# Attention scores and values in seven pieces of 64 keys, on the four quarters of the array

## The chip, the cores and the metric

The kernel runs on one NeuronCore of a Trainium2 chip. A core has TensorE (PE; its weight loads are shown apart as PEld), VectorE (DVE), ScalarE (ACT), GpSimd (POOL) and SyncE (SP, which here only issues transfers), all with their own instruction queues, and 16 DMA engines. The metric is the device time of one execution in microseconds; the times given are medians of several executions.

## The reference

Eight sequences of 448 tokens, 12 heads of 64. Attention with root-mean-square norms on q and k, then a SwiGLU feed-forward layer (FFN) on the joined heads:

```python
def _attn_ref(q, k, v, g_q, g_k):            # (8, 12, 448, 64), g: (64,)
    q_n, k_n = (rmsnorm(q, g_q), rmsnorm(k, g_k))
    scores = np.matmul(q_n, k_n.transpose(0, 1, 3, 2)) / np.sqrt(64)
    attn = np.exp(scores - np.max(scores, axis=-1, keepdims=True))
    attn = attn / (np.sum(attn, axis=-1, keepdims=True) + 1e-09)
    return np.matmul(attn, v)

def _moe_ref(x, w_gate, w_val, w_out, rms_g): # x: (3584, 768), d_ff 1536
    xn = x / rms * rms_g
    g = xn @ w_gate
    silu = g * (1.0 / (1.0 + np.exp(-g)))
    return silu * (xn @ w_val) @ w_out
```

All of it is float32 on the chip; the weights come as float64 and are converted by the kernel.

## The kernel before

Two versions of the computation are in the program: `safe_scores`, which runs unless a flag says that the scores could overflow, and `any_scores` behind the flag. Only `safe_scores` runs in the measurements, and only it is changed.

**Pairs.** Attention goes by pairs of heads, 48 pairs `g` in all, six for each sequence. A pair's 448 keys are 384 "full" ones, laid out as three blocks of 128 (`NK` = 3), and a rest of 64. q and k are turned by TensorE (`turn`, L531 and L535) into `qT` and `kT`, tiles of 128 partitions in which one head takes 64 partitions and the other head the other 64: `own(j)` and `across(j)` are these halves. In a 64-partition half the sum over the head's 64 numbers takes place.

**Scores, transposed.** `score` (L549) makes, for a block of 128 keys and one head, a tile of 128 keys by 448 queries: it contracts over 64 partitions (shape 64\*128 in the profile), so that the two heads use the upper and the lower half of the array. `Exp` on ACT (L553) writes `e`, and takes the key's norm `rs` as its scale per partition, since k itself is turned without it. `rests` does the last 64 keys with both heads in one tile (L579, shape 64\*64: each head has a quarter of the array, on the diagonal); these keys are normalised beforehand, so their `Exp` (L594) has no scale. There is no subtraction of a maximum: the scores are bounded by the norms.

**Values.** `av` is 128 partitions (two heads by 64) by 448 queries in one PSUM bank (pool `ps_m`, one buffer, shared with the turned tiles `tr`). `values` (L601) contracts over 128 keys and writes 64 rows (shape 128\*64), six matmuls a pair; `rests` adds the last keys' (L585) on the two quarters off the diagonal.

**Sums of e.** For the first seven pairs (`direct`) TensorE adds them all with a matrix of ones (L590, L614). From pair 7 on, POOL adds the tiles of each head into `es` (L559, L566), and TensorE adds over the keys with two matmuls (`den`, L614); ACT copies `den` (L621), DVE takes the reciprocal (L622) and multiplies `av` by it (L629) into `x`. The squares of x for the FFN's norm follow on ACT (L634) and POOL (L635).

**Norms of q and k.** `squares` (L488, ACT) for the pair after next, the sums on DVE (L491), `rms_qk` on POOL (L509, and L510, a power of -1/2, into `rs`), and `norm_q` on POOL (L515).

**Order.** Everything is ordered by hand: each engine runs its instructions in the order in which the program writes them. `pe(fn)` writes one step of TensorE's work, advances a counter, and then writes what `after(n, ...)` had put off to that step. The main loop at the end writes, for a pair g above 7: one burst of attention (scores of g with values and sums of g-1), and then the FFN's matmuls of an earlier sequence, item by item (`fill`), with the turns of g+1 between them. So ACT, DVE and POOL get attention work and FFN work in one mixed, fixed order. `load_pair` (three pairs ahead) and `load_v` (two ahead) are written on SP's queue among the transfers of the FFN's weights (L752, L801, L911).

**The FFN.** For the first sequence plain matmuls (L1363, L1101), while the weights are converted: ACT (L765, L766), DVE (L771 to L773) and POOL (L813), piece by piece; for later ones Strassen-like products (`quad`, L1004; outputs L1228 and L1296) in three PSUM buffers (`ps_f`), with sums on DVE and POOL and copies and tanh on ACT (L1023, L1046, L1315). The scores use four other PSUM buffers (`ps_s`), which a score's tile gives back after its `Exp`.

Of the kernel before, what the change touches and what calls it, by code (L numbers as in the profile page):

```python
# [8 lines left out]
F32 = mybir.dt.float32  # L9
# [3 lines left out]
ALU = mybir.AluOpType  # L13
ACT = mybir.ActivationFunctionType
# [4 lines left out]
B, H, S, D = 8, 12, 448, 64  # L19
DM, DF = H * D, 1536  # L20
NT, P = 4, 112
NK, REST = 3, S - 3 * 128
NPAIR = H // 2
# [312 lines left out]
def safe_scores(  # L336
# [20 lines left out]
    nc = tc.nc  # L357
# [16 lines left out]
    st = {}  # L374
# [4 lines left out]
    def after(n, fn):  # L379
        due.append((now["t"] + n, fn))  # L380

    def pe(fn):
        now["t"] += 1
        fn()
        for item in [d for d in due if d[0] <= now["t"]]:
            due.remove(item)
            item[1]()
# [6 lines left out]
    NG = B * NPAIR  # L394
# [4 lines left out]
    def own(j):  # L399
        return slice(j * D, (j + 1) * D)  # L400

    def across(j):
        return own(1 - j)
# [17 lines left out]
    def load_v(g):  # L421
        if g >= NG:
            return
        b, hp = divmod(g, NPAIR)
        vt = st["v", g] = v_pool.tile([128, 2, NK, D], F32, name="vt")
        nc.sync.dma_start(out=vt.rearrange("p h t d -> p h (t d)"),
                          in_=v[b, 2 * hp:2 * hp + 2, FULL].rearrange("h (p t) d -> p h (t d)", t=NK))


    def load_rests(b, i, engine):  # L430
# [44 lines left out]
    def direct(g):  # L475

        return g <= NPAIR

    def squares(g, i):

        if g >= NG:
            return
        n = 2 * NK
        if i == 0:
            st["ms", g] = small.tile([128, 2 * n], F32, name="ms")
        ms = st["ms", g]
        sq = tmp.tile([128, n * D], F32, name="sq", tag="sq", bufs=2)
        nc.scalar.activation(sq, st["qk", g][:, i], ACT.Square)  # L488

        def reduce():  # L490
            nc.vector.tensor_reduce(out=ms[:, i * n:(i + 1) * n], in_=sq.rearrange("p (n d) -> p n d", d=D), axis=AX_X, op=ALU.add)  # L491

        if g <= 1:

            return reduce, lambda: rms_qk(g, slice(i * n, (i + 1) * n))
        after(1, reduce)
        if i == 1:
            if g == 2:

                due[0:0] = [(now["t"] + 2, lambda: rms_qk(g)), (now["t"] + 2, lambda: norm_q(g))]  # L500
                return
            after(2, lambda: rms_qk(g))
            after(2, lambda: norm_q(g))

    def rms_qk(g, cols=slice(0, 4 * NK)):
        if ("rs", g) not in st:
# [5 lines left out]
    def norm_q(g):  # L512
        qn = st["qn", g] = qn_pool.tile([128, 2 * NK * D], F32, name="qn")
        for h in range(2):
            (nc.vector if g <= 2 else nc.gpsimd).tensor_tensor(  # L515
                qn.rearrange("p (t h d) -> p h t d", h=2, d=D)[:, 1 - h], st["qk", g][:, 0].rearrange("p (h t d) -> p h t d", h=2, d=D)[:, h],
                st["rs", g][:, h * NK:(h + 1) * NK].unsqueeze(2).to_broadcast([128, NK, D]), ALU.mult)

    def turn(g, i):

# [20 lines left out]
    def score(g, cs):  # L541

        qT, kT, rs = st["qT", g], st["kT", g], st["rs", g]
        sc = {}
        for c in cs:
            for j in range(2):
                r = across(j)
                ps = sc[c, j] = ps_s.tile([128, 512], F32, name="sc", tag="s")
                nc.tensor.matmul(ps[:, 0:S], lhsT=kT[r, c * 128:(c + 1) * 128], rhs=qT[r, :], start=True, stop=True)  # L549
        for (c, j), ps in sc.items():  # L550
            e = st["e", g, c, j] = e_pool.tile([128, S], F32, name="e")
            n = 2 * NK + c * 2 + 1 - j
            nc.scalar.activation(e, ps[:, 0:S], ACT.Exp, scale=rs[:, n:n + 1])  # L553


        def first():
            for j in range(2):
                es = st["es", g, j] = tmp.tile([128, S], F32, name="es", tag="es", bufs=4)
                nc.gpsimd.tensor_tensor(es, st["e", g, 0, j], st["e", g, 1, j], ALU.add)  # L559

        def more(of):
            for j in range(2):
                r = across(j) if of == "rest" else slice(0, 128)
                e = st["e", g, of] if of == "rest" else st["e", g, of, j]
                es = st["es", g, j]
                nc.gpsimd.tensor_tensor(es[r], es[r], e[r], ALU.add)  # L566

        if NK - 1 in cs and not direct(g):
            n = 3 if g == NPAIR + 1 else 2
            after(n, first)  # L570
            after(n + 2, lambda: more(2))
            after(n + 3, lambda: more("rest"))

    def rests(g):

        if g < NG:
            ps = ps_s.tile([128, 512], F32, name="sc", tag="s")
            for r in (own(0), own(1)):
                nc.tensor.matmul(ps[r, 0:S], lhsT=st["kT", g][r, LAST], rhs=st["qT", g][r, :], start=True, stop=True)  # L579
        if g:  # L580
            b, hp = divmod(g - 1, NPAIR)
            vr, e = st["vr", b][:, hp], st["e", g - 1, "rest"]
            av = st["av", g - 1] = ps_m.tile([128, 512], F32, name="av", tag="m")
            for j in range(2):
                nc.tensor.matmul(av[own(j), 0:S], lhsT=vr[across(j)], rhs=e[across(j)], start=True, stop=False,  # L585
                                 skip_group_check=True)
            if direct(g - 1):
                den = st["den", g - 1] = ps_f.tile([128, 512], F32, name="den", tag="f")
                for j in range(2):
                    nc.tensor.matmul(den[own(j), 0:S], lhsT=ones[across(j)], rhs=e[across(j)], start=True, stop=False,  # L590
                                     skip_group_check=True)
        if g < NG:
            e = st["e", g, "rest"] = e_pool.tile([128, S], F32, name="e")
            nc.scalar.activation(e, ps[:, 0:S], ACT.Exp)  # L594

    def values(g):

# [6 lines left out]
    def sums(g):  # L604


        b, hp = divmod(g, NPAIR)
        if direct(g):
            den, terms = st.pop(("den", g)), [[st["e", g, c, j] for j in range(2)] for c in range(NK)]
        else:  # L610
            den, terms = ps_s.tile([128, 512], F32, name="den", tag="s"), [[st.pop(("es", g, j)) for j in range(2)]]
        for i, pair in enumerate(terms):
            for j, term in enumerate(pair):
                nc.tensor.matmul(den[own(j), 0:S], lhsT=ones, rhs=term, start=not direct(g), stop=(i == len(terms) - 1),  # L614
                                 skip_group_check=True)
        rd = tmp.tile([128, S], F32, name="rd", tag="rd", bufs=1)
        if direct(g):
            nc.vector.reciprocal(rd, den[:, 0:S])
        else:

            nc.scalar.copy(rd, den[:, 0:S])  # L621
            nc.vector.reciprocal(rd, rd)  # L622
        half, c = divmod(hp, 3)
        if c == 0:
            st["x", b, half] = x_pool.tile([128, 3, S], F32, name="x")
        if hp == 0:
            st["ss", b] = tmp.tile([128, S], F32, name="ss", tag="ss", bufs=1)
        x, ss, av = st["x", b, half][:, c, :], st["ss", b], st.pop(("av", g))
        nc.vector.tensor_tensor(x, av[:, 0:S], rd, ALU.mult)  # L629
        soon = g == NPAIR - 1  # L630
        if hp == 0:
            after(3, lambda: nc.scalar.activation(ss, x, ACT.Square))
        else:
            after(1 if soon else 3, lambda: nc.scalar.activation(rd, x, ACT.Square))  # L634
            after(1 if soon else 4, lambda: (nc.gpsimd.tensor_tensor(ss, ss, rd, ALU.add), st.update({("summed", b): hp})))  # L635
        st.pop(("e", g, "rest"))
        for c in range(NK):
            for j in range(2):
                st.pop(("e", g, c, j))
        for key in ("qk", "v", "qT", "kT", "rs", "ms"):  # L640
            st.pop((key, g))


    def rms_x(b):
# [806 lines left out]
    ones = const.tile([128, D], F32, name="ones")  # L1451
# [71 lines left out]
    for g in range(NG + 1):  # L1523
# [45 lines left out]
                bound()  # L1569
            continue  # L1570

        pe(lambda: (rests(g), score(g, (0,)) if g < NG else None))
        if g == NPAIR + 1:
            pe(lambda: rms_x(0))
        pe(lambda: values(g - 1))
        load_v(g + 2)
        if g == NPAIR + 1:
            pe(lambda: score(g, (1,)))
            pe(lambda: norm_x(0))
            pe(lambda: score(g, (2,)))  # L1580
        pe(lambda: sums(g - 1))
        if g == NPAIR + 1:
            begin(0, 15)
        elif g < NG:
            pe(lambda: score(g, (1, 2)))
        st["block"] = now["t"]
        if hp:
            fill()
# [60 lines left out]
```

## Time and profile before

| | |
|---|---|
| median of 3 runs | 1577.93 us (1576.43 to 1578.04) |
| the profiled execution's own time | 1576.27 us |
| its span, first to last instruction | 1574.4 us |
| TensorE busy | 1544.4 us (98% of the span) |
| scores L549 / values L601 | 138.0 / 118.8 us of TensorE |
| DVE / POOL / ACT busy | 979.7 / 724.0 / 472.7 us |
| granted TensorE clock | 0.998 |

The profile is one execution, as the hardware recorded it. A group line gives line, engine, operation, output and inputs with shapes, the number of instructions, then busy time and mean duration of one in ns, then the engine's idle time in front of them with what ended it. Durations overlap where an engine is pipelined: matmuls that run side by side each show their full length. An f32 matmul shows as two passes, each with its own weight load, so L549's 288 matmuls are 576 rows. A timeline line gives start and length in us, and after "x" how many instructions were merged.

### The profile page before, as it was taken

The numbers are of one execution on the slowest core, as the hardware profiler recorded it, in microseconds if no ns is written. First come the engines' busy times: TensorE is split into PE (matmuls) and PEld (weight loads), VectorE is DVE, ScalarE is ACT, GpSimd is POOL, SyncE is SP. The second block draws the span as 40 slices with busy tenths as digits, with TensorE's granted clock in tenths as the row PEclk, the third lists the DMA queues.
The fourth block names the chain that finished last, engine by engine and source line by source line (L and its number), as shares of the span: only waits on it lengthen the run. The fifth ranks groups of instructions, "written<-read, shape, count | busy, mean of one in ns | idle before, by whom it ended". The sixth has DMA issues, their size and how long they took to land.

```text
span 1574.4 us, 23664 instructions
## 1 busy us (share of the span) xinstructions
PE 1544.4 (98%) x7916; PEld 1193.3 (76%) x7916; DVE 979.7 (62%) x1697; ACT 472.7 (30%) x955; POOL 724.0 (46%) x718
## 2 busy tenths in 40 slices
PE   8999999999999999999999999999999999999997
PEld 4344445777856888788887888668888788999997
DVE  6889889668754565854558544534549544573454
ACT  6746564232222222223222222322322222101000
POOL 6867887544423443464435643354544542021003
PEclk9999999999999999999999999999999999999999
DMA  7648574775789979785557855484556755578665
GB/s 208 214 142 266 169 236 139 251 238 195 252 264 292 307 225 301 237 253 172 153 163 214 267 160 156 142 262 144 151 146 210 233 172 141 161 259 261 175 196 186
DMA packets 313414, 327.10 MB, mean 208 GB/s; under 512 B 83652, under 2 KB 310212, under 8 KB 313284
## 3 DMA queue, kind: packets, MB, share of 16 engines
q1 hardware_dynamic: 312356, 325.30, 67.2%
q8 instruction: 65, 1.06, 0.3%
q14 instruction: 65, 0.53, 0.1%
q10 hardware_dynamic: 800, 0.20, 0.1%
q0 software_dynamic: 128, 0.00, 0.0%
HBM read 271.62 MB, written 53.77 MB: 207 GB/s over the span
## 4 chain that ended last, share of the span: by engine, by line
PE 75%; DVE 9%; issue 1%; DMA 1%; POOL 0%; ACT 0%; SPq 0%; DVEq 0%; POOLq 0%; ACTq 0%
PE ff L1004 42%; PE ff L1296 10%; PE sc L549 6%; PE av L601 5%; PE ff L1228 5%; PE sc L579 2%; PE den L614 2%; PE ff L1101 2%; PE tr L531 1%; DVE l L1171 1%; DVE top L772 1%; DVE rd L622 1%; DVE top L773 1%; DVE top L771 1%; DVE xs L684 1%
## 5 line engine op out<-in xcount | busy, mean ns | idle before, releaser
L1004 PE MATMUL ff<-x,w 128*128 128x224 f32 x1866 | 380.4, 354 | 0.0
L1004 PEld LDWEIGHTS ff<-x,w 128*128 128x128 f32 x1866 | 348.5, 190 | 15.6 <-issue 11.1
L559 POOL TENSOR_TENSOR es<-e 128x448 f32<-128x448 f32 x82 | 91.2, 1133 | 433.4 <-ACT e L553 433.4
L1004 PE MATMUL ff<-xs,w 128*128 128x224 f32 x1392 | 284.6, 353 | 3.2 <-DVE w L926 2.9
L1004 PEld LDWEIGHTS ff<-xs,w 128*128 128x128 f32 x1392 | 261.9, 190 | 4.9 <-issue 4.1
L566 POOL TENSOR_TENSOR es<-es,e 64x448 f32<-64x448 f32 (+1 forms) x164 | 197.3, 1213 | 6.3
L622 DVE RECIPROCAL rd<-rd 128x448 f32<-128x448 f32 x41 | 121.1, 2952 | 99.6 <-ACT rd L621 99.6
L553 ACT ACTIVATE e<-sc,rs 128x448 f32<-128x448 f32 x288 | 161.2, 634 | 49.8 <-PE sc L549 47.4
L549 PE MATMUL sc<-qT,kT 64*128 64x448 f32 x576 | 138.0, 572 | 1.9 <-ACT e L553 0.7
L601 PE MATMUL av<-e,vt 128*64 128x448 f32 x576 | 118.8, 548 | 0.0
L510 POOL TENSOR_TENSOR rs<-ms,mhalf 128x12 f32<-128x12 f32 (+1 forms) x50 | 115.9, 2318 | 4.2
L549 PEld LDWEIGHTS sc<-qT,kT 64*128 64x128 f32 x576 | 53.9, 185 | 82.5 <-issue 68.5
L1016 DVE TENSOR_TENSOR cc<-ff,u 128x448 f32<-128x448 f32 x84 | 52.4, 624 | 101.2 <-PE ff L1004 98.0
L1296 PE MATMUL ff<-w,l 128*128 128x192 f32 x578 | 110.0, 329 | 3.7 <-DVE l L1171 2.6
L1363 PE MATMUL ff<-x,w 128*128 128x448 f32 x288 | 111.8, 541 | 0.0
L1296 PEld LDWEIGHTS ff<-w,l 128*128 128x128 f32 x578 | 95.4, 190 | 9.7 <-DVE l L1171 4.5
L601 PEld LDWEIGHTS av<-e,vt 128*64 128x64 f32 x576 | 37.1, 136 | 75.6 <-issue 74.9
L1363 PEld LDWEIGHTS ff<-x,w 128*128 128x128 f32 x288 | 53.3, 190 | 50.8 <-issue 49.0
L1023 ACT ACTIVATE th<-c 128x224 f32<-128x224 f32 x42 | 16.3, 389 | 226.8 <-DVE c L1016 226.8
L1268 POOL TENSOR_TENSOR y<-y,c 128x384 f32<-128x384 f32 x10 | 12.2, 1216 | 151.9 <-DVE y L1337 143.0
L635 POOL TENSOR_TENSOR ss<-ss,rd 128x448 f32<-128x448 f32 x40 | 46.4, 1160 | 77.3 <-ACT rd L634 77.3
L813 POOL TENSOR_TENSOR w<-top,raw 128x384 int32<-128x384 int32 x63 | 66.5, 1069 | 25.6 <-issue 8.4
(199 smaller groups left out, 2337.0 us busy)
## 6 DMA issues: line engine op xcount, KB each, us to landing
w<-kept SPq DMA_DIRECT2D x512, 192.0 KB, 3.5
w<-kept_q SPq DMA_DIRECT2D x323, 192.0 KB, 3.5
w<-kept_o SPq DMA_DIRECT2D x136, 192.0 KB, 3.6
kept<-w SPq DMA_DIRECT2D x91, 192.0 KB, 3.7
kept_q<-w SPq DMA_DIRECT2D x57, 192.0 KB, 3.1
qk<-in_q_dram SPq DMA_DIRECT2D x48, 192.0 KB, 3.4
qk<-in_k_dram SPq DMA_DIRECT2D x96, 96.0 KB, 3.5
vt<-in_v_dram SPq DMA_DIRECT2D x48, 192.0 KB, 3.5
```

What stands on the lines that cost most here:

```text
L510: nc.gpsimd.tensor_tensor(st["rs", g][:, cols], ms, mhalf[:, cols], ALU.pow)
L549: nc.tensor.matmul(ps[:, 0:S], lhsT=kT[r, c * 128:(c + 1) * 128], rhs=qT[r, :], start=True, stop=True)
L553: nc.scalar.activation(e, ps[:, 0:S], ACT.Exp, scale=rs[:, n:n + 1])
L559: nc.gpsimd.tensor_tensor(es, st["e", g, 0, j], st["e", g, 1, j], ALU.add)
L566: nc.gpsimd.tensor_tensor(es[r], es[r], e[r], ALU.add)
L601: nc.tensor.matmul(av[own(j), 0:S], lhsT=vt[:, j, c], rhs=st["e", g, c, j], start=False, stop=(c == NK - 1), skip_group_check=True)
L622: nc.vector.reciprocal(rd, rd)
L813: nc.gpsimd.tensor_tensor(data(key).bitcast(I32), top, lo, ALU.add)
L1004: nc.tensor.matmul(bank[:, w * HT:(w + 1) * HT], lhsT=wt[:, c * 128:(c + 1) * 128], rhs=x[:, c, :], start=onto is None and w == c == 0, st ...
L1228: nc.tensor.matmul(ps, lhsT=left_o(b, which, LEFT_O[name], c), rhs=data(("wo", b, name, c)), start=first and c == 0, stop=c == NFP - 1, sk ...
L1296: nc.tensor.matmul(ps, lhsT=a[:, j, :], rhs=data(key)[:, n % 2 * HW:(n % 2 + 1) * HW], start=start and j == 0, stop=j == KG - 1, skip_grou ...
L1363: nc.tensor.matmul(bank[w][:, 0:S], lhsT=data(key)[:, c * 128:(c + 1) * 128], rhs=st["x", 0, half][:, c, :], start=half == c == 0, stop=ha ...
```

## The change

From pair 7 on, each pair's 448 keys are done in seven pieces of 64 keys (`PARTS`), as the rest was: for a piece, two score matmuls on the diagonal quarters (both heads in one PSUM tile), and two value matmuls of the pair before on the other quarters (`step`). Since a piece's `e` tile has keys of both heads on its partitions, the tile of sums `es` is one per pair, over all 128 partitions, and the two `den` matmuls (`totals`) contract over 64 partitions on the values' quarters. `totals` stands after two steps and writes the copy and the reciprocal; the multiplication (`weigh`) comes after the seventh step. The `Exp` has no scale; instead ACT multiplies k in place by `rs` (`norm_k`, six Copies of 128x64 for each pair, in two groups, three and four steps after the squares). v is loaded per head by two transfers, in an order that puts the keys of piece i and i + 3 of a block in the two halves. The first seven pairs (0 to 6) stay as they were, and their last half meets the new form at pair 7, whose scores are written without values beside them; after the last pair the values of pair 47 are written without scores.

The core of the diff; "..." marks what is left out:

```diff
@@ load_v
-        nc.sync.dma_start(out=vt.rearrange("p h t d -> p h (t d)"),
-                          in_=v[b, 2 * hp:2 * hp + 2, FULL].rearrange("h (p t) d -> p h (t d)", t=NK))
+        rows = vt.rearrange("p h t d -> p h (t d)")
+        if direct(g):
+            nc.sync.dma_start(out=rows, in_=v[b, 2 * hp:2 * hp + 2, FULL].rearrange("h (p t) d -> p h (t d)", t=NK))
+            return
+        for h in range(2):
+            nc.sync.dma_start(out=rows[across(h)], in_=v[b, 2 * hp + h, FULL].rearrange("(f p t) d -> p f (t d)", f=2, t=NK))
@@ squares
             after(2, lambda: norm_q(g))
+            if not direct(g):
+                for half in range(2):
+                    after(3 + half, lambda half=half: norm_k(g, half))
...
+    def norm_k(g, half):
+        for n in range(NK * half, NK * (half + 1)):
+            block = st["qk", g][:, 1, n * D:(n + 1) * D]
+            nc.scalar.activation(block, block, ACT.Copy, scale=st["rs", g][:, 2 * NK + n:2 * NK + n + 1])
@@ score: the POOL sums of two es tiles are gone (now later_sums)
...
@@ sums: for the direct pairs alone; its second half is weigh
-        rd = tmp.tile([128, S], F32, name="rd", tag="rd", bufs=1)
-        if direct(g):
-            nc.vector.reciprocal(rd, den[:, 0:S])
-        else:
-            nc.scalar.copy(rd, den[:, 0:S])
-            nc.vector.reciprocal(rd, rd)
...
+    PARTS = 2 * NK + 1
+
+    def keys_of(i):
+        at = i % NK * 128 + i // NK * D if i < 2 * NK else NK * 128
+        return slice(at, at + D)
+
+    def scores(g, i):
+        ps = ps_s.tile([128, 512], F32, name="sc", tag="s")
+        for r in (own(0), own(1)):
+            nc.tensor.matmul(ps[r, 0:S], lhsT=st["kT", g][r, keys_of(i)], rhs=st["qT", g][r, :], start=True, stop=True)
+        return ps
+
+    def exps(g, i, ps):
+        e = st["e", g, i] = e_pool.tile([128, S], F32, name="e")
+        nc.scalar.activation(e, ps[:, 0:S], ACT.Exp)
+
+    def weighted(g, i):
...
+        for j in range(2):
+            r = across(j)
+            vt = st["vr", b][r, hp] if i == PARTS - 1 else st["v", g][r, i // NK, i % NK]
+            nc.tensor.matmul(st["av", g][own(j), 0:S], lhsT=vt, rhs=st["e", g, i][r], start=i == 0, stop=i == PARTS - 1,
+                             skip_group_check=True)
+
+    def step(g, i):
+        ps = scores(g, i) if g < NG else None
+        weighted(g - 1, i)
+        if ps is not None:
+            exps(g, i, ps)
+
+    def totals(g):
+        es, den = st.pop(("es", g)), ps_s.tile([128, 512], F32, name="den", tag="s")
+        for j in range(2):
+            nc.tensor.matmul(den[own(j), 0:S], lhsT=ones[across(j)], rhs=es[across(j)], start=True, stop=True)
+        rd = st["rd"] = tmp.tile([128, S], F32, name="rd", tag="rd", bufs=1)
+        nc.scalar.copy(rd, den[:, 0:S])
+        nc.vector.reciprocal(rd, rd)
+
+    def later_sums(g, n):
+        def first():
+            st["es", g] = tmp.tile([128, S], F32, name="es", tag="es", bufs=2)
+            nc.gpsimd.tensor_tensor(st["es", g], st["e", g, 0], st["e", g, 1], ALU.add)
+            more(2)
+        def more(*parts):
+            for i in parts:
+                nc.gpsimd.tensor_tensor(st["es", g], st["es", g], st["e", g, i], ALU.add)
+        after(n, first)
+        after(n + 2, lambda: more(3, 4))
+        after(n + 3, lambda: more(5, 6))
@@ main loop, pairs above 7 (and the values after the last pair)
-        pe(lambda: (rests(g), score(g, (0,)) if g < NG else None))
...
-        pe(lambda: values(g - 1))
-        load_v(g + 2)
...
-        pe(lambda: sums(g - 1))
...
-        elif g < NG:
-            pe(lambda: score(g, (1, 2)))
+            pe(lambda: [step(g, i) for i in (0, 1)])
+            pe(lambda: (totals(g - 1), step(g, 2)))
+            load_v(g + 2)
+            pe(lambda: [step(g, i) for i in (3, 4)])
+            pe(lambda: ([step(g, i) for i in (5, 6)], weigh(g - 1, 2)))
+            if g < NG:
+                later_sums(g, 2)
```

## The prediction

> **What bounds the kernel now.** I read the page first: busy shares and the costliest groups. TensorE is busy nearly all the time and no other engine comes near it.
>
> ```profile
> PE 1544.4 (98%) x7916; PEld 1193.3 (76%) x7916; DVE 979.7 (62%) x1697; ACT 472.7 (30%) x955; POOL 724.0 (46%) x718
> ...
> L549 PE MATMUL sc<-qT,kT 64*128 64x448 f32 x576 | 138.0, 572 | 1.9 <-ACT e L553 0.7
> L601 PE MATMUL av<-e,vt 128*64 128x448 f32 x576 | 118.8, 548 | 0.0
> ```
>
> The reader is to see that the two groups which the change cuts up (scores L549, values L601) hold 257 us of TensorE time and that almost nothing is waited for in front of them. So what counts is how much TensorE time one pair's attention takes, and whether anything new makes TensorE wait. Next, the timeline of TensorE for one middle pair (start, us, line, operation, number of passes; an f32 matmul shows as two passes):
>
> ```profile
> 600.08 0.59 PE L579 MATMUL sc<-qT,kT 64*64 64x448 f32 x2
> 600.10 0.59 PE L585 MATMUL av<-e,vr 64*64 64x448 f32 x2
> 600.51 0.54 PE L579 MATMUL sc<-qT,kT 64*64 64x448 f32 x2
> 600.52 0.54 PE L585 MATMUL av<-e,vr 64*64 64x448 f32 x2
> 601.00 1.02 PE L549 MATMUL sc<-qT,kT 64*128 64x448 f32 x4
> 601.95 2.48 PE L601 MATMUL av<-e,vt 128*64 128x448 f32 x12
> 604.25 0.92 PE L614 MATMUL den<-es,ones 128*64 128x448 f32 x4
> 605.11 1.77 PE L549 MATMUL sc<-qT,kT 64*128 64x448 f32 x8
> 606.81 0.46 PE L1004 MATMUL ff<-x,w 128*128 128x224 f32 x1
> ```
>
> The burst lasts 606.81 - 600.08 = 6.73 us; 38 of the 40 bursts from pair 8 on last 6.73 to 6.75. Its first 0.92 us already do what the change wants everywhere: scores on the diagonal quarters and values on the others start within 0.02 us of each other, twice. The weight loads of the values inside the burst give the pace of a set (passes that run side by side), and an earlier burst shows quarters following quarters:
>
> ```profile
> 602.38 0.14 PEld L601 LDWEIGHTS av<-e,vt 128*64 128x64 f32 x2 [0.23 <-issue]
> 602.75 0.14 PEld L601 LDWEIGHTS av<-e,vt 128*64 128x64 f32 x2 [0.23 <-issue]
> 603.13 0.14 PEld L601 LDWEIGHTS av<-e,vt 128*64 128x64 f32 x2 [0.23 <-issue]
> ```
>
> ```profile
> 75.78 0.59 PE L579 MATMUL sc<-qT,kT 64*64 64x448 f32 x2
> 75.79 0.59 PE L585 MATMUL av<-e,vr 64*64 64x448 f32 x2
> 76.20 0.54 PE L579 MATMUL sc<-qT,kT 64*64 64x448 f32 x2
> 76.22 0.54 PE L585 MATMUL av<-e,vr 64*64 64x448 f32 x2
> 76.59 0.92 PE L590 MATMUL den<-e,ones 64*64 64x448 f32 x4
> 77.44 2.48 PE L601 MATMUL av<-e,vt 128*64 128x448 f32 x12
> ```
>
> A set takes 0.375 us once the shape stays the same (602.38, 602.75, 603.13). The first set of a shape takes 0.42 (75.78 to 76.20), and the last before another shape 0.85 - 0.375 = 0.475 (two den sets, 76.59 to 77.44). Each change of shape thus costs about 0.15 us, and a burst has five.
>
> **The change, part by part.** *Burst.* Today's work is 2 + 2 + 6 + 2 + 4 = 16 sets: 6.0 us plus 0.73 for the changes of shape. After, seven steps of two sets each, and two den sets on the values' quarters: again 16 sets on the busier quarters, all 64x64. So the array does no less work; only the changes of shape go: 0.42 + 14 x 0.375 + 0.475 = 6.15. I take 6.2, a gain of 0.53 per burst. From both sides: if only the switches inside went and a set of four took the 0.41 to 0.42 of the first one, 16 x 0.415 = 6.64 (gain 0.09); at 16 x 0.375 = 6.0 the gain is 0.73.
>
> The rule that speaks against this is in the Trainium skill, TensorE: Matmul & The Clock Gate, "Packing small matmuls — row/col tiling": a weight load overlaps running matmuls only when its row group differs. In the new burst both row groups always run, so by it each set would show a load; with this case's 64x64 loads of 0.131 us, 16 x (0.375 + 0.131) = 8.1 us, and 40 bursts would cost 55 us more. The trace speaks against it: the den load that uses the same rows is issued at 76.22, while L579's passes of 76.20 to 76.74 run, and den's first pass starts at 76.59, 0.39 after.
>
> *ACT in the burst.* Seven exps as before (0.52 to 0.58 apart), the den copy (0.53) and at most one or two tanh: about 5 us of 6.2. Score tiles use four PSUM buffers; by these rows the den copy ends about 3.4 us into the burst and the step that reuses its buffer starts at about 4.2. It is covered with 0.75 us to spare.
>
> *Sums.* POOL's six adds per pair (1.13 to 1.21 each) stay six. The reciprocal (2.95) moves from the burst's end into it, so it costs nothing and x comes about 2 us earlier. The PSUM bank of av is held to the end of the burst instead, and the next transposes come over 2 us later.
>
> *v.* Two transfers of 96 KB instead of one of 192: 41 more issues on SP at 0.4 to 0.6 us. v's buffer is now free only after step 5 (5.4 us into the burst; before, 4.2), so SP stands at that issue about 1 us longer, and the weight loads queue behind it. About 20 weight slots are filled ahead, 1.1 us of matmuls each, against 3.5 us to land: nothing.
>
> *k scaled by ACT.* Six Copies of 128x64 per pair, 41 pairs. Nearest rows: 128x64 Square 0.256 us, 128x192 Copy 0.318; some 0.25 each, 62 us in all, on an engine 70% idle. But ACT runs in order, and these wait for POOL's rs. Laying POOL's rs ends (5.2 to 12.6 us after the pair's last Square) against the ACT instructions on either side, ACT would stand 183 us in all, mostly where it was idle. What stands behind and is needed: (a) pair 7, while the first pairs run:
>
> ```profile
> 68.56 2.37 POOL L510 TENSOR_TENSOR rs<-ms,mhalf 128x12 f32<-128x12 f32 x1
> ```
>
> ```profile
> 72.71 3.26 ACT L553 ACTIVATE e<-sc,rs 128x448 f32<-128x448 f32 x6 [2.84 <-PE sc L549]
> ```
>
> ACT is at the k scaling at 66.7, rs comes at 70.9, six copies end at 72.4, then the six conversion steps that ran in that gap (2.7 us) push the exps from 72.7 to 75.1: 2.4 us, which TensorE waits for its PSUM. (b) In three places of the quad output (first at 654.2) the copy L1315 comes 4.4 us late; a bank has about 3 us to spare: 1.5 each, 4.5 in all (0 to 9). Other late instructions there are tanhs of 0.4 to 2.5 us, on tiles with more room.
>
> *Edges.* Pair 7's scores run alone: three pieces go from two sets to four, 3 x 0.75 = 2.25, of which 0.75 falls into TensorE's idle 1.02 us before L661: 1.5. The last pair's values run alone too: 4.06 us become 6.2: +2.1.
>
> *Before 285 us.* There DVE is busy about 89% and the chain runs through the conversion of the weights (the last piece ends at 279.2, TensorE needs it at about 280), so six bursts' gain (3.2) is taken back there and the early losses (2.4 + 1.5) are met only in part: +2 at 285 us (-3 to +8, if ACT's waits push the conversions). At 300 to 420 us TensorE waits 2.9 us for derived weights; being earlier gives about 1 back.
>
> **Sum**, against the profiled execution's 1576.27: 34 x -0.53 = -18.0; +2; +1; +4.5; +2.1: **-8.4**, 1567.9. The median of the runs lies 1.66 above the profiled execution, so 1569.5; the early term is likelier below +2 than above, as half of the bursts' gain there may survive: I say 1568.
>
> **Rivals.** *A, the other side: ACT's wait at the k scaling reaches TensorE.* One queue, one place, once per pair. By the rows above instructions directly behind it are 68 us late in all; I put 4.5 + 2.4 of it on the path. From about 15 us on the path the gain is gone; at one half (34) it is 1576.3 - 8.4 - 4.5 + 34 - 2 = 1595, at a third 1584. For it: POOL's rs is late in nearly every pair. Against: ACT idles 268 us today in front of L1023 and L1315 alone, for TensorE, so most of the new waits lie in time that it has.
>
> *B, TensorE's instructions come too slowly.* A burst grows from 72 to 120 loads and passes in less time. The densest long row today, transposes, takes 0.109 us for two, 54.7 ns each: 120 x 0.0547 = 6.56, a gain of 0.17: 34 x -0.17 + 9.6 = +3.8, 1581.7. Slower from 54 ns or so on. Against: 8 loads and 4 passes start within 0.07 us at 600.08.
>
> *C, weight loads or the four streams do not overlap over a long row:* the 8.1 us above, 1576.3 + 55 + 9 = 1640. Only two sets in a row of four quarters are seen today.
>
> *D, nothing gained:* sets at 0.415 (gain 0.09): -3.1 + 9.6 - 4 (early) gives 1577 to 1583.
>
> **Chances.** As forecast 0.64, with its own range 1557 to 1576; A 0.13, B 0.09, C 0.05, D 0.09. The measurement tells about 0.2% (3 us) from no change. Faster: the forecast but its upper edge, 0.62, and a few hundredths of the rest: 0.66. Within 0.2%: 0.08. Slower: A, B, C and half of D: 0.26. Low end: all early gain kept, no ACT wait, sets at 0.37: 1576.3 - 21 + 2 = 1557, less 1. High end: A at a third and B, 1585. The range leaves out C and the worse half of A.
>
> **What the profile after would show.** Bursts of 6.1 to 6.3 us from first score to next ff pass, with one 64*64 score group and one av group interleaved; idle "issue" in front of their loads down; no "sc <- ACT e" beyond 2 us in all. L553's scaled exps gone outside the first seven pairs; six Copies a pair near 0.25 us, with ACT waiting for POOL rs some 180 us; TensorE idle between 280 and 1360 us up by under 8. The forecast is wrong if bursts exceed 6.6 us, or if TensorE idles over 15 us more than before.

## The result, and the profile after

| | before | after |
|---|---|---|
| median of 20 runs each, same chip | 1576.89 us (1575.96 to 1578.20) | 1576.74 us (1573.10 to 1578.67) |
| profiled execution's own time | 1576.27 us | 1576.01 us |
| TensorE busy | 1544.4 us | 1531.4 us |
| ScalarE (ACT) busy | 472.7 us | 518.3 us |

The ratio is 0.9997, with a 95% interval of 0.9991 to 1.0004: no change. The forecast was 1568. TensorE is busy 13.0 us less, and idles 12.4 us more: 42.4 us of its span of 1573.8 where it was 30.0 of 1574.4.

First the page's busy line, and three of the costliest groups (idle time of the engine in front of them behind the second bar).

```profile
PE 1531.4 (97%) x8900; PEld 1198.3 (76%) x8900; DVE 982.2 (62%) x1697; ACT 518.3 (33%) x1201; POOL 725.6 (46%) x718
```

```profile
L638 PE MATMUL sc<-qT,kT 64*64 64x448 f32 x1176 | 236.9, 546 | 7.7 <-ACT e L643 3.6 <-DVE kT L553 2.8 <-ACT rd L669 1.3
L653 PE MATMUL av<-e,vt 64*64 64x448 f32 x984 | 203.7, 545 | 0.0
...
L531 ACT ACTIVATE qk<-qk,rs 128x64 f32<-128x64 f32 x246 | 65.0, 336 | 180.5 <-POOL rs L518 180.5
```

Scores and values now run side by side, so their times in the list overlap and do not add up. In front of the k scaling (L531) ACT stands 180.5 us for POOL's `rs`; 183 had been forecast. Next, the timeline of TensorE for one middle pair:

```profile
607.57 0.59 PE L638 MATMUL sc<-qT,kT 64*64 64x448 f32 x2
607.59 0.59 PE L653 MATMUL av<-e,vt 64*64 64x448 f32 x2
608.00 0.54 PE L638 MATMUL sc<-qT,kT 64*64 64x448 f32 x2
...
609.13 0.54 PE L638 MATMUL sc<-qT,kT 64*64 64x448 f32 x2
609.14 0.54 PE L667 MATMUL den<-es,ones 64*64 64x448 f32 x2
609.50 0.54 PE L638 MATMUL sc<-qT,kT 64*64 64x448 f32 x2
...
612.90 0.92 PE L653 MATMUL av<-e,vr 64*64 64x448 f32 x4
613.75 0.65 PE L1048 MATMUL ff<-x,w 128*128 128x224 f32 x2
```

The burst lasts 613.75 - 607.57 = 6.18 us, against 6.73. After the first set (0.43) the sets follow each other by 0.37 to 0.38 us to the end. So the burst gave what was forecast. The time went elsewhere, and early. The timeline of ACT, DVE and TensorE while pair 7 gets ready (in brackets the engine's idle time before the instruction, and what ended it):

```profile
73.01 1.54 ACT L531 ACTIVATE qk<-qk,rs 128x64 f32<-128x64 f32 x6 [4.16 <-POOL rs L518]
...
75.03 1.17 DVE L815 TENSOR_SCALAR xs<-xs 128x384 f32<-128x384 f32 x1 [3.62 <-ACT xs L809]
...
77.11 3.21 ACT L567 ACTIVATE e<-sc,rs 128x448 f32<-128x448 f32 x6
...
77.77 1.57 PE L563 MATMUL sc<-qT,kT 64*128 64x448 f32 x4 [2.26 <-ACT e L567]
```

ACT stands 4.16 us at the head of its queue. Behind it are six conversion steps (L809, L810), for which DVE stands 3.62 us, and behind those the exps for which TensorE stands 2.26.

**A ledger.** To place the loss, I took from each profile when four bursts begin: the first of all, pair 8's (the first full one in the new form), pair 14's (near 286 us, where the weight conversion has just ended) and the last. Before: 10.83, 116.83, 286.31, 1347.62 us, end 1574.4. After: 12.91, 124.56, 296.32, 1345.11, end 1573.8. In the table the first burst's lateness is taken off the next two columns; all entries are us against before.

| kernel | first burst | lag at pair 8 | lag at pair 14 | pair 14 to last burst | last burst to end |
|---|---|---|---|---|---|
| after | +2.1 | +5.7 | +7.9 | -12.5 | +1.9 |
| e2_no_k | +0.3 | +0.7 | -1.7 | -16.3 | +2.4 |
| e3_k_alone | +1.7 | +5.0 | +9.9 | +3.8 | 0.0 |
| e1_k_later | 0.0 | +1.9 | +2.7 | -16.8 | +3.4 |
| e4_k_pool | +0.2 | +0.7 | +2.8 | -14.5 | +1.7 |
| e5_first_two | +0.1 | +1.9 | +6.0 | -12.9 | +2.6 |
| e8_first_eight | +1.9 | +1.9 | +2.7 | -11.5 | +4.3 |
| e7_pool_then_late | +1.7 | +0.7 | +0.3 | -15.0 | +2.1 |
| e9_fill_nine | +0.3 | +5.7 | +9.8 | -12.1 | +2.6 |

The first column is no property of a kernel: the instructions ahead of the first burst are the same in all. Each row is one execution, and it holds the stretches of 3.41 us in which TensorE's granted clock stood at half between the first burst and the last: none in before and e2, one in e1, e4, e7 and e8, two in after and e3, three in e5 and e9. Half its length, 1.7 us, is the most that one can cost. In the ledger without the first column, after is 2.7 us ahead of before; the forecast was 8.4.

### The profile page after: what moved, and what is told of

Same layout as the page of the kernel before. It is cut to its first block, busy times and chain, and to the rows that moved or that the text cites. A ratio compares the mean times of both kernels' runs of the same rounds, so it can differ in the third digit from the quotient of the medians.

```text
span 1573.8 us, 25892 instructions
## 1 busy us (share of the span) xinstructions
PE 1531.4 (97%) x8900; PEld 1198.3 (76%) x8900; DVE 982.2 (62%) x1697; ACT 518.3 (33%) x1201; POOL 725.6 (46%) x718
## 4 chain that ended last, share of the span: by engine, by line
PE 74%; DVE 5%; issue 3%; POOL 2%; DMA 1%; ACT 0%; SPq 0%; POOLq 0%; DVEq 0%; ACTq 0%
PE ff L1048 41%; PE sc L638 11%; PE ff L1340 9%; PE ff L1272 5%; PE av L653 2%; PE ff L1145 2%; PE ff L1407 2%; PE tr L545 1%; POOL es L681 1%; DVE l L1215 1%; POOL rs L518 0%; DVE raw L1189 0%; DVE w L970 0%; DMA kept_o<-w 0%; DVE raw L1215 0%
## 5 line engine op out<-in xcount | busy, mean ns | idle before, releaser
L1048 PEld LDWEIGHTS ff<-x,w 128*128 128x128 f32 x1866 | 348.5, 190 | 16.8 <-issue 11.3
L681 POOL TENSOR_TENSOR es<-es,e 128x448 f32<-128x448 f32 x205 | 243.8, 1189 | 18.0 <-ACT e L643 4.9
L638 PE MATMUL sc<-qT,kT 64*64 64x448 f32 x1176 | 236.9, 546 | 7.7 <-ACT e L643 3.6
L653 PE MATMUL av<-e,vt 64*64 64x448 f32 x984 | 203.7, 545 | 0.0
L643 ACT ACTIVATE e<-sc 128x448 f32<-128x448 f32 x294 | 154.8, 545 | 124.9 <-PE sc L638 107.1
L676 POOL TENSOR_TENSOR es<-e 128x448 f32<-128x448 f32 x41 | 47.3, 1155 | 280.2 <-ACT e L643 280.2
L638 PEld LDWEIGHTS sc<-qT,kT 64*64 64x64 f32 x1176 | 76.4, 134 | 126.4 <-issue 94.2
L531 ACT ACTIVATE qk<-qk,rs 128x64 f32<-128x64 f32 x246 | 65.0, 336 | 180.5 <-POOL rs L518 180.5
L1060 DVE TENSOR_TENSOR u<-ff,p 128x448 f32<-128x448 f32 x42 | 26.2, 624 | 87.5 <-PE ff L1048 85.5
```

The source lines that it names most:

```text
L638: nc.tensor.matmul(ps[r, 0:S], lhsT=st["kT", g][r, keys_of(i)], rhs=st["qT", g][r, :], start=True, stop=True)
L653: nc.tensor.matmul(st["av", g][own(j), 0:S], lhsT=vt, rhs=st["e", g, i][r], start=i == 0, stop=i == PARTS - 1, skip_group_check=True)
L681: nc.gpsimd.tensor_tensor(st["es", g], st["es", g], st["e", g, i], ALU.add)
L1048: nc.tensor.matmul(bank[:, w * HT:(w + 1) * HT], lhsT=wt[:, c * 128:(c + 1) * 128], rhs=x[:, c, :], start=onto is None and w == c == 0, st ...
L1060: nc.vector.tensor_tensor(add[name], ps[:, 0:S], add[other], ALU.add)
```

## The experiments

Two theories stood at the start. W: ACT's wait for `rs` at the k scaling, in its fixed order, took the gain. V: it is the weight conversion that sets the time up to 285 us, whatever ACT does.

**e1_k_later: the scaling later in the same order.**

```diff
-                    after(3 + half, lambda half=half: norm_k(g, half))
+                    after(6 if g <= NPAIR + 2 else 6 + half, lambda half=half: norm_k(g, half))
```

> The changed kernel with the scaling of k written three steps later on ACT's queue (six steps after the squares; for pairs 7 and 8 behind the exps of the step that they stood in front of). Theory W (ACT's wait for POOL's rs at the k scaling is what took the bursts' gain: about 6 us at pairs 7 and 8 and in their halved clock, a few us up to 285 us, about 6 us after): 1564 to 1570, ACT's wait for rs in front of the copies down from 180 us to under 60, TensorE's first burst with pair 7 back from 12.8 us to about 10.5. Rival V (the conversion of the weights bounds the stretch up to 285 us whatever ACT does): at 285 us no earlier than the changed kernel, only the later 3 to 6 us come back, 1571 to 1574.

1567.70 us (1566.01 to 1569.41), ratio 0.9942 (0.9929 to 0.9956). The same instructions, 9 us faster than where the change has them. ACT's waits for `rs`, after and then here (us in all, times, longest):

```profile
ACT qk L531 <- POOL rs L518: 180.5, 40, 8.9
```

```profile
ACT qk L531 <- POOL rs L518: 49.4, 12, 5.7
```

**e2_no_k: no scaling of k at all.** The norm of k is left out (the scale of q is made 1 instead of 8, so that the numbers stay small).

```diff
-            if not direct(g):
-                for half in range(2):
-                    after(3 + half, lambda half=half: norm_k(g, half))
...
-        nc.vector.scalar_tensor_tensor(gqk, gq, D**0.5, gk, ALU.mult, ALU.mult)
+        nc.vector.scalar_tensor_tensor(gqk, gq, 1.0, gk, ALU.mult, ALU.mult)
```

> The changed kernel without the scaling of k: the part of the norm of k is left out for pairs 7 to 47 (the gains are made smaller by a constant so that the exps stay finite), so its time is that of the new form with no work and no wait of ACT for k. Theory W: the full price of the k scaling, 1561 to 1567, and 10 us earlier than the changed kernel at 285 us less the two or so that the conversion takes back. Rival V: 1570 to 1573.

1561.55 us (1560.24 to 1562.81), ratio 0.9902 (0.9887 to 0.9917). The rest of the change is worth 15 us, and all of it went into scaling k.

**e3_k_alone: the scaling of k without the rest of the change**, put into the kernel before; its exps lose their scale from pair 7 on.

```diff
+            if not direct(g):
+                for half in range(2):
+                    after(3 + half, lambda half=half: norm_k(g, half))
```

> The kernel before with the scaling of k by ACT alone (same place as in the change; the exps of pairs 7 to 47 without their scale), bursts as before. Theory W: 10 to 15 us slower than before, 1587 to 1592, with the same 2.3 us wait of TensorE for the exps near pair 7 and a stretch at half clock behind it. Rival V: the bursts' own time is not what was lost, so little changes: 1577 to 1581.

1591.46 us (1590.46 to 1591.68), ratio 1.0089 (1.0075 to 1.0102): +14 us, with bursts of 6.73 us as before (37 of 40). ACT waits 181.7 us for `rs` in 40 places, as after. In the ledger the lag at pair 14, +9.9, is close to the 9.6 by which after stands behind e2_no_k there. So the price does not come from the new bursts. Behind pair 14 the time from one burst to the next is as before, but for three places where it is 1.24 us longer; they come back below.

**e4_k_pool: k scaled by POOL**, in one multiplication a pair, right behind q's; POOL has made `rs` itself just before, so nothing waits.

```diff
-                for half in range(2):
-                    after(3 + half, lambda half=half: norm_k(g, half))
+                after(2, lambda: norm_k(g))
...
+        k = st["qk", g][:, 1].rearrange("p (n d) -> p n d", d=D)
+        nc.gpsimd.tensor_tensor(k, k, st["rs", g][:, 2 * NK:4 * NK].unsqueeze(2).to_broadcast([128, 2 * NK, D]), ALU.mult)
```

> The changed kernel with k scaled by POOL, one multiplication of 128x384 right behind the one of q, so that no engine waits for another on its account; POOL gets about 1.1 us more a pair. Theory W: ACT's waits are gone, 1565 to 1571. Rival V: POOL and the conversions behind it are the bound up to 285 us, so that the early loss stays or grows: 1573 to 1578.

1567.29 us (1566.36 to 1568.09), ratio 0.9937 (0.9924 to 0.9951). Its group of 41 multiplications:

```profile
L528 POOL TENSOR_TENSOR qk<-qk,rs 128x384 f32<-128x384 f32 x41 | 36.1, 881 | 0.0
```

These four speak for W. V keeps a part: in e4, where ACT waits for nothing at the scaling, there is still a lag of 2.8 us at pair 14, where e2 has a lead of 1.7. Some of the scaling's price up to there is work, not waiting.

**e5_first_two and e8_first_eight: which pairs pay.** Only pairs 7 and 8, or 7 to 14, are delayed.

```diff
-                    after(3 + half, lambda half=half: norm_k(g, half))
+                    after(6 if g <= NPAIR + 2 else 3 + half, lambda half=half: norm_k(g, half))
```

> The changed kernel with norm_k of pairs 7 and 8 alone six steps after their squares; the others stay where the change has them. Theory (ScalarE's wait for rs at the first two pairs, and the half clock behind it, cost what the forecast missed): relative to before, pair 8's burst started 5.65 us late in the changed kernel and 1.92 us late with all pairs delayed, so 3.7 us come back: 1573.0 (1572 to 1574), against 1576.7 of the changed kernel. Rival (these microseconds are no cost of their own, the weight conversion sets when the burst at 286 us can start): the gain is used up by 286 us, 1576 to 1577.

```diff
-                    after(3 + half, lambda half=half: norm_k(g, half))
+                    after(6 if g <= NPAIR + 2 else 6 + half if g <= 2 * NPAIR + 2 else 3 + half, lambda half=half: norm_k(g, half))
```

> The changed kernel with norm_k of pairs 7 to 14 delayed, as in e1_k_later, and the later ones where the change has them. If the loss lies in two parts (up to 286 us: +7.9 of the changed kernel against +2.7 with all delayed, so 5.2; behind it 4.3), this run takes back the first alone: 1571.5 (1570.5 to 1572.5). If the early part is all: 1567.7, as e1_k_later. If it is the later part: 1576.

1573.45 us (1571.95 to 1576.94), ratio 0.9977 (0.9968 to 0.9987), and 1571.76 us (1570.89 to 1573.52), ratio 0.9964 (0.9951 to 0.9978). Both fell where the ledger put them, at 1573.0 and 1571.5. So by the ratios, from after to e1_k_later: 3.2 us for two pairs, 2.0 for the next six, 3.5 for the 33 after them; the intervals of the two runs overlap, so the 2.0 is not clear of the noise. One detail looks like V: in e5's profile 4.1 us are lost between pair 8 and pair 14 (after: 2.3). It is not V's chain. Of the 1.8 us more, 1.7 lie in pair 9's burst, 7.97 us long where after's has 6.27, and there e5's clock stood at half from 148.17 to 151.59.

How a later pair pays is seen in the timeline of after, up to the start of pair 9's burst:

```profile
147.54 0.82 ACT L531 ACTIVATE qk<-qk,rs 128x64 f32<-128x64 f32 x3 [6.86 <-POOL rs L518]
...
148.91 0.84 DVE L815 TENSOR_SCALAR top<-top 128x384 f32<-128x384 f32 x1 [1.72 <-ACT top L809]
...
152.05 0.54 DVE L553 COPY kT<-tr 128x384 f32<-128x384 f32 x1
152.65 0.59 PE L638 MATMUL sc<-qT,kT 64*64 64x448 f32 x2 [2.75 <-DVE kT L553]
```

ACT stands 6.86 us for `rs`, DVE stands 1.72 us for a conversion step that ACT does behind it, and TensorE stands 2.75 us for the copy of kT that DVE has behind that step. e5, where pair 9's scaling comes as early, has the same wait of TensorE; e8 has none there, and its step from pair 8's burst to pair 9's is 2.05 us shorter than after's.

**e6_fill and e9_fill_nine: was it TensorE's wait, and the half clock behind it?** In after, TensorE's granted clock fell to a half from 79.1 to 82.6 us, just behind its wait of 2.26 us; I took that for the reason why the lag at pair 8 was 5.7 and not 3.9. Matmuls without use keep TensorE busy through the wait.

```diff
+    def fill_idle(n):
+        for _ in range(n):
+            nc.tensor.matmul(st["spare"][:, S:512], lhsT=ident, rhs=ident[:, 0:512 - S], start=True, stop=True,
+                             skip_group_check=True)
...
-            pe(lambda: score(g, (1, 2)))
+            if g == NPAIR - 1:
+                pe(lambda: (score(g, (1, 2)), fill_idle(18), st.pop("late")()))
+            else:
+                pe(lambda: score(g, (1, 2)))
```

(`st["spare"]` is the PSUM tile of pair 4's sums; its reciprocal, `late`, is written behind the fill. e9_fill_nine has 9 in place of 18.)

> The changed kernel with 18 matmuls of 64 columns in unused columns of a sum's bank between pair 5's last scores and pair 6's first, where TensorE stood 2.26 us for an exp behind norm_k. They compute nothing that is used. If the idle time is what halved the granted clock from 79.1 us for 3.4 us: the granted clock from 78 to 84 us is 1.0, pair 7's first 2 sets are 0.375 us apart and not 0.75, and burst 8 starts 1.7 us sooner; 1575.0. Rival (the half clock has another cause): the clock still falls to 0.5 at about 79 us, and the time is that of the changed kernel, 1576.7, or up to 0.5 above.

1578.94 us (1576.18 to 1582.52), ratio 1.0011 (1.0001 to 1.0020). The 18 took 4.23 us, twice what I had reckoned, so that pair 6's scores now stood behind them; but the clock did not fall. So nine (what the expectations call the bursts of pairs 7 and 8 here, 14.53 us apart, are the last keys' scores of pairs 5 and 6):

> As e6_fill with 9 matmuls in place of 18. There each took 0.23 us, twice what was reckoned, and they ended 1.5 us after the exp that pair 6's first scores wait for; the clock stayed at 1.0 from 72 to 88 us. Nine take 2.1 us and end before it. If the idle time halves the clock: granted clock 1.0 from 78 to 84 us, pair 8's burst begins 1.3 to 1.7 us sooner after pair 7's than in the changed kernel (14.53 us there), 13.0; 1575.3 (1574.5 to 1576). Rival (the work of the 18 hid it by moving the rest): half clock again near 79 us, 14.5, 1576.7.

1577.93 us (1574.74 to 1580.80), ratio 1.0002 (0.9993 to 1.0012): nothing came back. First the busy times by stretch of after, then of e9 (columns: PE, PEld, DVE, ACT, POOL, then the granted clock, DMA share and GB/s):

```profile
78.00:81.00 3.00, 3.00 (x13) 1.76 (x12) 2.96 (x3) 3.00 (x7) 0.33 (x1) 0.69 0.96 321
81.00:84.00 3.00, 2.88 (x12) 0.81 (x12) 2.97 (x6) 1.67 (x4) 0.58 (x1) 0.74 0.19 45
```

```profile
78.00:81.00 3.00, 1.46 (x10) 0.51 (x7) 2.97 (x3) 2.00 (x5) 0.00 (x0) 1.00 0.73 220
81.00:84.00 3.00, 2.88 (x16) 1.09 (x18) 1.49 (x4) 1.01 (x2) 2.11 (x3) 1.00 0.00 0
```

And the timeline of e9 there (L615 is the fill; L828 and L822 are after's L815 and L809):

```profile
73.32 1.18 DVE L828 TENSOR_SCALAR xs<-xs 128x384 f32<-128x384 f32 x1 [3.62 <-ACT xs L822]
...
73.72 2.22 PE L615 MATMUL den<-ident 128*128 128x64 f32 x18
76.11 1.53 PE L563 MATMUL sc<-qT,kT 64*128 64x448 f32 x4 [0.17 <-ACT e L567]
...
77.36 2.95 DVE L604 RECIPROCAL rd<-den 128x448 f32<-128x448 f32 x1
...
81.12 0.97 PE L577 MATMUL av<-e,vr 64*64 64x448 f32 x4 [1.66 <-DVE kT L551]
```

The clock stays at 1.0, as expected, and the last keys' scores of pair 6 begin 0.74 us sooner after pair 5's (13.79 us against 14.53). Then TensorE waits 1.66 us for DVE, and from pair 5's to the broadcast of the first sequence's scales (L705 in after) it is 34.58 us against after's 34.55. My cause was wrong: the half clock followed the loss, and cost nothing here. (e9's profile has a stretch at half clock of its own from 152.28 us, behind pair 8's start; it is in the whole time, not in this comparison.) What is left is the other thing that ACT's wait holds up. DVE stands 3.62 us for the conversion steps in both kernels, and its reciprocal, the product and the copy of kT behind them come that much late. That DVE's wait alone makes the loss is read from e9's order; no run freed DVE and kept TensorE waiting. The wait ahead of pair 9's burst, shown above, goes the same way, and there the trace names DVE.

**e7_pool_then_late: both remedies.** POOL scales k for pairs 7 and 8, ACT for the others, twelve and thirteen steps after the squares.

```diff
-                for half in range(2):
-                    after(3 + half, lambda half=half: norm_k(g, half))
+                if g <= NPAIR + 2:
+                    after(2, lambda: norm_k(g, None))
+                else:
+                    for half in range(2):
+                        after(12 + half, lambda half=half: norm_k(g, half))
```

> k of pairs 7 and 8 scaled by GpSimd right behind q, as in e4_k_pool, and of the later pairs by ScalarE 12 and 13 steps after the squares. Pair 8's burst started 0.5 us late with GpSimd and 1.9 late with e1_k_later, which still waited 49.4 us for rs in 12 places: 1.4 less than e1_k_later's 1567.7 gives 1566.3, and up to 1 less where those waits cost something: 1565.3 to 1567. Rival (ScalarE's copies come so late that the transposes of k wait for them, or the six copies hold a later exp): 1568 to 1572, with TensorE waiting for qk in its list of waits.

1565.55 us (1563.91 to 1566.03), ratio 0.9922 (0.9909 to 0.9936), 12 us below before, the fastest of those that scale k. ACT's group for the k scaling has no idle time in front of it any more:

```profile
L538 ACT ACTIVATE qk<-qk,rs 128x64 f32<-128x64 f32 x234 | 63.3, 341 | 0.0
```

The copies take nearly the same 65 us of ACT as after; it was the waits. The lag at pair 14 is down to 0.3 us. What still separates this kernel from e2_no_k, 0.2% or 3 us with intervals that touch, may be the work itself, on ACT and on POOL; in the profiles 1.0 us of it lies in the step from pair 17 to pair 18, where this kernel's clock stood at half (389.09 to 392.51) and e2's did not. No run separates the two.

## Why the prediction was wrong, point by point

- **Burst, right.** 32 of the 40 bursts from pair 8 on take 6.17 to 6.18 us where 6.2 was forecast, five more 6.26 to 6.40, and three with a wait inside 7.71, 7.80 and 10.20: a gain of 0.55 for 0.53. Sets of four quarters follow at the full pace, so rivals B (instruction supply), C (weight loads) and D (0.415 us a set) fell. In the changed kernel the loads of each set, which fill rows that the running passes use, stand beside the passes:

```profile
609.50 0.14 PEld L638 LDWEIGHTS sc<-qT,kT 64*64 64x64 f32 x2 [0.22 <-issue]
609.52 0.14 PEld L653 LDWEIGHTS av<-e,vt 64*64 64x64 f32 x2
609.88 0.14 PEld L638 LDWEIGHTS sc<-qT,kT 64*64 64x64 f32 x2 [0.22 <-issue]
```

  Loads at 609.50 and 609.88, passes 0.37 to 0.38 us apart: nothing is added. The Trainium skill's rule that a weight load overlaps only when its row group differs (TensorE: Matmul & The Clock Gate, "Packing small matmuls — row/col tiling") would have made 8.1 us of the burst; the measurement decides against it.
- **ACT in the burst, sums, v: right.** From pair 14 to the last burst after gains 12.5 us; the forecast's terms for it are -18.0 + 1 + 4.5 = -12.5. The 4.5 us for ACT's lateness at the quad output are found in three places, as forecast: from the bursts at 639.55, 829.71 and 1187.71 us to the next it takes 0.6 us longer than in the kernel before, and in e1_k_later 0.75 less than there: 4.0 us in all. That fits with the 3.5 us that e1_k_later gains on e8_first_eight. The first of them, in the timeline of ACT, DVE and TensorE:

```profile
664.06 0.82 ACT L531 ACTIVATE qk<-qk,rs 128x64 f32<-128x64 f32 x3 [8.93 <-POOL rs L518]
664.79 0.29 ACT L1359 COPY th<-ff 128x192 f32<-128x192 f32 x1
...
665.12 0.36 DVE L1360 TENSOR_TENSOR cc<-ff,th 128x192 f32<-128x192 f32 x1 [2.00 <-ACT th L1359]
...
665.53 1.24 PE L1340 MATMUL ff<-w,h 128*128 128x192 f32 x6 [1.06 <-DVE cc L1360]
```

  Here too the wait reaches TensorE by way of DVE. That the sum is met so closely is partly luck: from the bursts at 381.02 and 541.27 us to the next it takes 0.9 and 1.0 us longer than before, where most pairs gain 0.55, and only the first of these was in the forecast (+1).
- **Edges, right in sum.** The last pair's values: +1.9 for +2.1. Pair 7's scores alone: about +0.7, for 1.5, by e2_no_k and e4_k_pool, in which nothing waits for a scaling there.
- **"ACT would stand 183 us in all, mostly where it was idle": the first half right (180.5), the price not.** The scaling cost 14 to 15 us in all (e3 against before, after against e2); the forecast had 6.9 on the path.
- **The step that failed: "Before 285 us: +2".** It measured +7.9, just inside its own bounds of -3 to +8. Two things in it were wrong. For pair 7 I followed ACT's wait to the exps and to TensorE's PSUM (2.4 us; TensorE did wait 2.26) and not to DVE: the six conversion steps that I had seen behind the wait feed the engine that I had called 89% busy, and DVE lost 3.6 us that nothing there made up. The six steps of DVE behind the wait also took 4.0 us (75.03 to 79.06) where before they took 2.7 (69.27 to 71.97); why is not shown. So its reciprocal began 5.0 us later, counted from the first burst, and with pair 7's scores (0.7) that made +5.7 at pair 8, not 3.9. Then I gave pairs 9 to 14 no price of their own, though their waits push the same conversion: the step from pair 8's burst to pair 9's is 2.35 us longer than before, by the wait for kT shown above. The forecast also left out the half clock. The longest burst of the stretch, 10.20 us at 207 us in place of 6.17, has it:

```profile
208.91 0.56 ACT L809 ACTIVATE top<-raw 128x384 f32<-128x384 f32 x1 [5.34 <-POOL w L857]
...
212.45 1.01 PE L638 MATMUL sc<-qT,kT 64*64 64x448 f32 x2 [2.23 <-ACT e L643]
...
213.25 0.96 PE L638 MATMUL sc<-qT,kT 64*64 64x448 f32 x2
214.00 0.96 PE L638 MATMUL sc<-qT,kT 64*64 64x448 f32 x2
```

  The exps, from 211.88 us, stand behind conversion steps that wait for POOL's `w`, not for `rs`; the same burst has such a wait of 1.60 us in e2_no_k, which scales nothing, and there it takes 8.00 us. In after the wait is 2.23 us, and behind it the clock is at half from 212.25 to 215.67: sets follow by 0.75 us in place of 0.375. That is some 1.7 of the 4.0 us that this burst has too many.

  After loses another 2.3 us from pair 8 to pair 14, where e2_no_k wins 2.4; the forecast had 1.9 won.
- **Rival A was the truth, at its least.** It named the queue and the point, "from about 15 us on the path the gain is gone"; 14 to 15 us were on it. I gave it 0.13, priced it at 23 to 34 us, and let ACT's 70% of idle time speak against it. That share is a mean: from 10 to 285 us ACT was busy 158 of 275 us in the kernel before, and at the places shown the work behind its waits was awaited.
- **The sum.** Forecast -8.4; the ledger without the first burst gives -2.7, and 5.9 of the difference of 5.7 is the early term. A further 2.1 us were lost in the profiled execution ahead of the first burst. The medians lie 0.15 us apart.
- **The tests I set were too wide.** 37 of 40 bursts stayed below 6.6 us and TensorE idled 12.4 us more, not 15, and still the forecast was wrong: against a sum of 8 a bound of 15 tells nothing. One sign did show: the scores wait 3.6 us for ACT's `e` in all, where 2 was to be the most.

## What to carry to other kernels

When an instruction that waits is put into an in-order queue, list everything that the queue holds behind it and follow each to its own consumer; the one that hurts may sit on a third engine that has no slack, and not on the one in front of you. Price the stretch with the least slack apart, pair by pair, and take the busy share of that stretch rather than the engine's mean. A scaling whose input comes late is put where the input has long been there, or on the engine that makes the input: here the same copies at another place in the same queue were worth 9 us.

## What the runs showed of the hardware

- **The half clock comes on a grid.** In the trace's records of the granted clock every stretch at 0.5 before a run's last matmuls lasts 3.41 us and begins a whole number of 3.41 us after the clock's first rise. Over the eleven profiles, every step of that grid in which TensorE idled 1.97 us or more (2.05 in after at 75.7, 2.05 in e9 at 148.9, 2.64 in e5 at 390.5) was followed by one at half clock, none with 1.80 or less was, and between them it went both ways (1.82 in e3 yes, 1.83 and 1.86 in after no). Whether a wait of about 2 us halves the clock thus depends on how it falls on the grid: the wait of some 2.75 us ahead of pair 9's burst left the clock alone in after and was followed by half clock in e5, e6 and e9. The Trainium skill (TensorE: Matmul & The Clock Gate, "What's actually happening") has the window of 3413 ns, but asks for a whole idle one; here some 58% of one were enough. The runs of the changed kernel spread over 5.6 us where those of before spread over 2.2, and such windows may be why; that was not tested.
- **The clock's first rise varies with the same instructions.** In the eleven profiles the full clock came for good at 4.8 to 6.0 us (six, before among them) or at 10.2 to 11.0 us (four, after among them, and e8, which had lost it again at 7.6), ahead of any instruction that differs; the first burst began at 10.8 to 11.2 or at 12.5 to 12.9 us. Some 1.7 us of a profiled execution thus say nothing of the kernel. No kernel was profiled twice.
- **Half the columns, nearly the same time.** Nine matmuls of 64 columns with a 128x128 weight load for each pass took 2.22 us, 0.247 each, at full clock; in the same run the five warm-up matmuls of 128 columns at 9.06 us took 1.28, 0.256 each, also at full clock.
